# A relu² attention and gated feed-forward kernel on one core: two score buffers and four accumulation banks throughout in place of a shared pair, and an identity matrix zeroed on another engine

## The chip, the cores and the metric

The kernel runs on one core of a Trainium2 chip. A time is the device time of one execution in microseconds (us). "Span" is the time from the first to the last instruction in a profiled execution, without what lies around it.

## The reference

Attention with squared relu for 8 batches of 12 heads, 448 tokens and 64 numbers per head, then a gated feed-forward block over all 3584 tokens:

```python
scores = scale * np.matmul(q, k.transpose(0, 1, 3, 2))      # (8, 12, 448, 448), scale 1/8
attn = np.maximum(scores, 0.0) ** 2 / S                     # S = 448
attn_out = np.matmul(attn, v)
...
x = attn_out.transpose(0, 2, 1, 3).reshape(3584, 768)
g = x @ w_gate                                              # (768, 1536)
gelu = 0.5 * g * (1.0 + erf(g * inv_sqrt2))
val = x @ w_val                                             # (768, 1536)
out = (gelu * val) @ w_out                                  # (1536, 768)
```

## The kernel before

**Tiles of the array.** Every matmul of `mm` (line 160) uses a quarter of TensorE's array, 64 rows by 64 columns. Four can run at once: the lower and the upper half of the rows, each with two column halves. The sum over the upper rows goes on top of that over the lower rows in the same bank of PSUM (the accumulation memory, eight banks), so a bank is first written by "lower" matmuls (plan queue `PE0`), then by "upper" ones (`PE1`). `wait_lower` (line 163) makes the first upper matmul of a bank wait for the last lower one.

**Work per batch**, in the order of the data:

- q and k are loaded by GpSimd's queue (`load_qk`, line 203) and transposed. Batches 0 and 1 use TensorE transposes with the identity matrix `ident` (`add_transposes`, line 358) and a copy by VectorE (line 377). Batches 2 to 7 use a VectorE copy (`qkr`, line 259) and DMA transposes on SyncE's queue (line 263).
- 21 score units per batch (`add_scores`, line 394). A unit's matmuls fill one score buffer `sp` of two banks, ScalarE applies relu (`rl`, line 421) and VectorE squares it (`attnT`, line 427).
- 6 value banks per batch (`add_values`, line 455): attention times v into a bank `ff`, which VectorE scales into `xT` (line 483).
- 24 gate and value banks (`add_gate_value`, line 515): 12 lower and 12 upper matmuls into a bank `ff`. A gate bank is read by gelu on ScalarE (`gel`, line 534), a value bank by VectorE's product (`uT`, line 539).
- 7 output banks per batch on the average (`add_out`, line 568): 24 lower and 24 upper matmuls into a bank `ff`, copied to `osb` (line 594, ScalarE; VectorE for the last tile) and stored by SyncE.

Attention of a batch is mixed with the feed-forward work of the batch before it.

**What sets the order.** The kernel is a plan: each piece is an `Op` with an engine, a cost, the Ops that it needs and a place. `run_plan` (line 23) walks through the queues in planned time and emits the instructions. Lower work has a fixed order (sorted by its place `at`); upper work is sorted by when the lower work ahead of it ends (lines 725 to 742). Both halves are emitted into one instruction queue of TensorE, which executes in order: an instruction that waits holds up all behind it. Until planned time 30, `fill` (line 324) puts dummy matmuls into planned gaps.

**Buffers.** The eight banks are two score buffers of two banks (`psS[0]`, `psS[1]`) and four single banks (`psF`, `FB = 4`). A user of a `psF` bank depends on the reader of the fourth user before it (`ring_dep`, line 338). That holds until the last score unit of batch 1 has been placed (line 442). From then on `next_scores` (line 312) gives all scores to `psS[0]`, each unit waiting for the reader of the one before. `next_bank` (line 298) counts the `ff` users in sixes: four take `psF` banks, the fifth (`n == 0`) allocates one tile of two banks from `psS[1]` and takes its first half, the sixth (`n == 1`) takes the second half of the same tile:

```python
            if half == 0:
                spare_tile[:] = [psS[1].tile([128, 2, 512], f32, name="ff", tag="S")]
            return spare_tile[0][:, half, :]
```

In the plan the fifth user waits for the readers of the pair before, and the sixth for nothing. The tile framework adds its own waits between instructions that touch a tile, in the order in which they are emitted.

**The start.** VectorE clears `warm` and `table` (lines 146, 149); TensorE runs 20 dummy matmuls on `warm` (line 748). GpSimd issues the loads of heads 0 and 1 of q and k, then makes `ident` (`make_identity`, line 628: a memset and a select, lines 197 and 199 of its own file), then issues the loads of heads 2 and 3, and so on (lines 624 to 646).

Of the kernel before, what the change touches and what calls it, by code (L numbers as in the profile page):

```python
# [88 lines left out]
def kernel(  # L89
# [10 lines left out]
    nc = tc.nc  # L100
    f32 = mybir.dt.float32
# [20 lines left out]
    SB = 2  # L122
    FB = 4
# [13 lines left out]
    apool = ctx.enter_context(tc.tile_pool(name="apool", bufs=12))  # L137
    gpool = ctx.enter_context(tc.tile_pool(name="gpool", bufs=3))
    opool = ctx.enter_context(tc.tile_pool(name="opool", bufs=4))
    psS = [ctx.enter_context(tc.tile_pool(name=f"psS{i}", bufs=1, space=bass.MemoryType.PSUM))  # L140
           for i in range(SB)]
    psF = ctx.enter_context(tc.tile_pool(name="psF", bufs=FB, space=bass.MemoryType.PSUM))

    ident = const.tile([128, 128], bf16)
    warm = const.tile([128, 512], bf16)
    nc.vector.memset(warm[:, :], 0.0)

    table = const.tile([128, 2], f32)
    nc.vector.memset(table[:, :], 0.0)
# [135 lines left out]
    ring = [warm_op]  # L285

    in_bank = []
    units, wide, spare, spare_tile = [], [], [[]], []

    def new_bank(reader, shape=(128, 512), dtype=f32, half=None):  # L290
        if half is not None:
            if half == 0:
                spare_tile[:] = [psS[1].tile([128, 2, 512], f32, name="ff", tag="S")]
            return spare_tile[0][:, half, :]
        in_bank.append(reader)
        return psF.tile(list(shape), dtype, name="ff", tag="F")

    def next_bank():

        n = wide[0] % (FB + 2) - FB if wide else -1  # L300
        if wide:
            wide[0] += 1
        if n < 0:
            return None, ring_dep()
        if n == 0:
            spare.append([])
        return n, spare[-2] if n == 0 else []

    def bank_read(half, reader):
        (ring if half is None else spare[-1]).append(reader)  # L310

    def next_scores():

        if wide:
            return 0, units[-1:]
        n = len(units)
        return n % SB, units[n - SB:n - SB + 1]

    def scores_read(n, reader):
        units.append(reader)  # L320
        if n == 1:
            spare[0] = [reader]

    def fill(t0, t1):

# [12 lines left out]
    def ring_dep():  # L338
        return [ring[-FB]] if len(ring) >= FB else []
# [14 lines left out]

    att, xT, last_s = {}, {}, {}
    t_op, relu_op, sq_op, o_op, x_op = {}, {}, {}, {}, {}

    def add_transposes(at, b, m, rs):

        box = {}  # L360

        def emit(r):
            if b == 0:
                t = new_bank(t_op[b, m, r], [128, SC, 2 * P], bf16)
            else:
                if not box:
                    box["S"] = psS[n].tile([128, 2, 1024], bf16, name="sp", tag="S")
                t = box["S"][:, r, 0:SC * 2 * P].rearrange("d (c x) -> d c x", c=SC)
            box[r] = t
            src = qk16[b].rearrange("p (h c d) -> p h c d", c=SC, d=D)  # L370
            for c in range(SC):
                for j in range(2):
                    nc.tensor.transpose(t[HALF[j], c, :], src[:, 2 * (2 * m + r) + j, c, :],  # L373
                                        ident[:, :], tile_position=(0, P * j))

        def emit_copy(r):
            nc.vector.tensor_copy(by_group(qkT_tile(b))[:, m, :, r, :], box[r])

        n, last = next_scores() if b else (0, [])
        for r in rs:  # L380
            have = [*(head_op[b, 2 * m + r, i] for i in range(2)), *(last if b else ring_dep())]
            lo = Op("PE0", 0.5, lambda r=r: emit(r), have, lag=0.2)
            hi = Op("PE1", 0.4, lambda: None)
            hi.after = lo
            t = t_op[b, m, r] = Op("DVE", 0.54, lambda r=r: emit_copy(r),
                                   [lo, last_s.get(b - 2)], lag=0.2, prio=1)
            DVE.append(t)
            if not b:
                ring.append(t)
            both(at, [(lo, hi)])  # L390
        if b:
            scores_read(n, t)

    def add_scores(at, b, u):

# [3 lines left out]
        prs = (2 * m, 2 * m + 1) if tail else (2 * m + (w > VC - 1),)  # L399
        cl = w if w < VC else w - VC  # L400
        box = {}
        n, free = next_scores()

        def emit(j, pr):
            if not box:
                box[0] = psS[n].tile([128, 2, 512], f32, name="sp", tag="S")
            sp = box[0]
            t = by_group(qkT_tile(b))[HALF[j], m, :, pr % 2, :]
            for i in range(2):
                if tail:  # L410
                    n0 = (pr % 2) * S // 2
                    qs = t[:, :, i * P // 2:(i + 1) * P // 2]
                    mm(sp[HALF[i], j, n0:n0 + S // 2].rearrange("k (c p) -> k c p", c=SC),
                       t[:, VC - 1, HALF[1]], qs, j, i, True, True)
                else:
                    mm(sp[HALF[i], j, 0:S].rearrange("k (c p) -> k c p", c=SC),
                       t[:, cl + i * VC, HALF[1]], t[:, :, HALF[0]], j, i, True, True)
# [12 lines left out]
            have = [t_op[b, m, pr % 2] for pr in prs]  # L430
        else:
            have = tr_op[b, m]
        have = [*have, *free]
        ops = [[Op(f"PE{j}", 0.095 if tail else 0.189, lambda j=j, pr=pr: emit(j, pr), have, lag=0.24)
                for pr in prs] for j in range(2)]
        last_s[b] = ops[1][-1]
# [1 line left out]
        n_a = len(sq_list)  # L438
        sq = Op("DVE", 0.54, emit_sq, [relu, *att_free[n_a - 12:n_a - 11]] if n_a >= 12 else [relu],
                lag=0.2, prio=2)  # L440
        scores_read(n, relu)
        if (b, u) == (EARLY - 1, NU - 1):
            wide.append(0)
        sq_list.append(sq)
        att_free.append(None)
        for pr in prs:
# [8 lines left out]
    def add_values(at, b, pr):  # L455
# [1 line left out]

        order = ([0, 3, 1, 2] if pr % 2 else [0, 1, 2, 3], [3, 0, 1, 2])
        last = (b, pr) == (0, NPAIR - 1)
        half, free = next_bank()  # L460

        def emit(i, w):
            if pr == 0 and i == 0 and w == 0:
                xT[b] = xpool.tile([128, KC, S], bf16, name="xT", tag="xT")
            if not box:
                box[0] = new_bank(x_op[b, pr], half=half)
            if (i, w) == (1, VC - 1) or last and (i, w) == (0, 1):
                wait_lower(box)
            for j in range(2):
                o = box[0][HALF[j], 0:S]  # L470
                a = att[b, pr, w][HALF[i], j, :]
                if w < VC - 1:
                    ins = mm(o, v16[b][HALF[i], 2 * pr + j, w + i, :], a, i, j,
                       i == 0 and w == 0, i == 1 - last and w == VC - 2)
                else:
                    ins = mm(o.rearrange("d (c p) -> d c p", c=SC)[:, :, i * P // 2:(i + 1) * P // 2],
                       v16[b][HALF[i], 2 * pr + j, (1 - i) * (VC - 1), :],
                       a[:, (pr % 2) * S // 2:(pr % 2 + 1) * S // 2].rearrange(
                           "k (c p) -> k c p", c=SC), i, j, False, False)
            box[1] = ins  # L480

        def emit_copy():
# [2 lines left out]
        sqs = sq_op[b, pr]  # L485
        have = [head_op[b, pr, 2], head_op[b, pr, 3]]
        ops = [[Op(f"PE{i}", 0.189 if w < VC - 1 else 0.095, lambda i=i, w=w: emit(i, w),
                   [*have, sq_of[b, pr, w], *(free if i == 0 else ())], lag=0.24)
                for w in order[i]]
               for i in range(2)]  # L490
        o_op[b, pr] = ops[1 - last][-1]
# [1 line left out]
            att_free[n_a] = o_op[b, pr]  # L493
        x_op[b, pr] = Op("DVE", 0.54, emit_copy, [o_op[b, pr]], lag=0.2, prio=1)
        DVE.append(x_op[b, pr])
        bank_read(half, x_op[b, pr])
        if last:
            ops[1][0].after = ops[0][1]
            for o, p in zip(ops[1], ops[1][1:]):
# [15 lines left out]
    def add_gate_value(at, b, fc, g):  # L515
# [1 line left out]
        i, o = divmod(fc * 128, WCH)  # L517
        w = (wg, wv)[g][i]
        box = {}
        half, free = next_bank()  # L520

        def emit(r, dc):
            if not box:
                box[0] = new_bank(done, half=half)
            if r == 1 and dc == 0:
                wait_lower(box)
            for j in range(2):
# [8 lines left out]
        def emit_mult():  # L536
            if fc == 0:
# [2 lines left out]
                uT[b][:, fc, :], gel.pop((b, fc))[:, :], box[0][:, 0:S], op=ALU.mult).ins  # L540

        ops = [[Op(f"PE{r}", GS, lambda r=r, dc=dc: emit(r, dc),
                   [w12_op[i][g], x_op[b, dc], *(free if r == 0 and dc == 0 else ())], lag=0.24)
                for dc in range(KC)] for r in range(2)]
        if g == 0:
            done = gel_op[b, fc] = Op("ACT", 0.55, emit_gelu, [ops[1][-1]], lag=0.06, prio=0)
# [1 line left out]
        else:  # L548
# [3 lines left out]
            if b + 2 < B and b:  # L552
# [7 lines left out]
                elif fc > 6:  # L560
                    h0 = 2 * (fc - 7)
                    load_v(b + 2, h0, h0 + 4, [done])
        bank_read(half, done)
        if (b, fc) == (0, 0):
            at = [PLACE5 - 0.5 + 0.1 * g] * 3 + [0.01 * g] * 3
        then(at, GS, *ops, done)
# [1 line left out]
    def add_out(at, t, g):  # L568

        box = {}  # L570
        half, free = next_bank()
        last = 2 * t + 2 == B * SC
        bounds = (0, OGS, OGS + OGS // 2, 2 * OGS) if last else (0, OGS, 2 * OGS)
        cols = slice(bounds[g], bounds[g + 1])
# [3 lines left out]

        def emit(r, fc):
            if not box:  # L580
                box[0] = new_bank(cp, half=half)
            i, o = divmod(fc, WOG)
            if r == 1 and fc == 0:
                wait_lower(box)
# [11 lines left out]
        def emit_store(j, engine, cols):  # L596
# [3 lines left out]

        ops = [[Op(f"PE{r}", step, lambda r=r, fc=fc: emit(r, fc),
                   [wo_op[fc // WOG], *(u_op[b, fc] for b, _ in chunks),
                    *(free if r == 0 and fc == 0 else ())], lag=0.24)
                for fc in range(FC)] for r in range(2)]

        cp = Op("DVE" if last else "ACT", 0.48, emit_copy, [ops[1][-1]], prio=1)
        bank_read(half, cp)
        (DVE if last else ACT).append(cp)
        if t == 0:
            load_qk(2, g, H - 4, H, [cp])  # L610
# [13 lines left out]
    for h0, h1 in ((0, 2), (2, 4), (4, 8), (8, 12)):  # L624
        load_qk(0, 0, h0, h1)
        load_qk(0, 1, h0, h1)
        if h0 == 0:
            POOL.append(Op("POOL", 0.6, lambda: make_identity(nc, ident)))
        if h0 > 2:
            load_v(0, h0 - 4, h1 - 4)  # L630
    load_v(0, 8, 12)
# [77 lines left out]


    def emit_filler():
        t = psS[0].tile([128, 2, 512], f32, name="sp", tag="S")
        for _ in range(2):
            mm(t[HALF[0], 0, 0:P], warm[HALF[0], 0:P], warm[HALF[0], 0:P], 0, 0, True, True)
            mm(t[HALF[1], 0, 0:P], warm[HALF[0], 0:P], warm[HALF[0], 0:P], 0, 1, True, True)
# [68 lines left out]
```

## Time and profile before

| | us |
|---|---|
| three runs | 458.68, 459.71, 460.55 |
| median | 459.71 |
| the profiled execution, its own time | 458.68 |
| its span | 456.7 |
| last matmul ends | 452.64 |
| TensorE busy, of the span | 426.3 |
| VectorE, ScalarE, GpSimd busy | 213.2, 224.3, 73.6 |
| granted TensorE clock | 1.00 in every stretch |

The profile's page sums up one execution. Views of its trace say more: the waits (which engine sat idle, on whose instruction, how long in all, how often, longest), the timeline (instructions in order of time, equal ones merged, with the idle time before them in brackets), groups by form and a table of stretches of time. `ff`, `sp` and the others are the names of tiles; line numbers are those of the kernel before. A matmul row's length includes its way through the array, so rows that follow each other overlap.

### The profile page before, as it was taken

How to read it: one execution, taken by the hardware profiler on the slowest of the kernel's cores; microseconds unless marked ns; L12 is line 12 of the kernel's file. 1: busy time of each engine (PE TensorE's matmuls, PEld its weight loads, DVE VectorE, ACT ScalarE, POOL GpSimd, SP SyncE). 2: the span in 40 equal slices, each digit the busy share in tenths (PEclk: the TensorE clock that was granted, in tenths of full speed). 3: DMA queues.
4: the chain of work that ended last, by engine and by line, in shares of the span. 5: the costliest groups of instructions: out<-in, count | busy, mean ns of one | idle time of the engine just before them, and what ended most of it. 6: DMA issues, size and time to landing. Idle time of an engine off the chain costs nothing.

```text
span 456.7 us, 19664 instructions
## 1 busy us (share of the span) xinstructions
PE 426.3 (93%) x9090; PEld 351.9 (77%) x9090; DVE 213.2 (47%) x347; ACT 224.3 (49%) x320; POOL 73.6 (16%) x120
## 2 busy tenths in 40 slices
PE   8999999999998999998999899989899989999896
PEld 3559679788887888786888788877689877876685
DVE  3967663466434564355534555345543545212201
ACT  4956652656554554554555555554455555221120
POOL 7654302313001130012200121011210000000000
PEclk9999999999999999999999999999999999999999
DMA  8999999988954688637863377544964100220024
GB/s 108 199 197 198 205 187 150 184 103 104 115 91 60 78 112 121 93 43 106 109 141 64 43 106 110 126 62 66 111 119 99 28 1 3 53 56 3 1 72 106
DMA packets 75281, 44.91 MB, mean 98 GB/s; under 512 B 36160, under 2 KB 71744, under 8 KB 75200
## 3 DMA queue, kind: packets, MB, share of 16 engines
q0 software_dynamic: 37152, 24.39, 41.9%
q1 hardware_dynamic: 37888, 19.08, 21.9%
q8 instruction: 71, 1.16, 1.1%
q10 hardware_dynamic: 160, 0.20, 0.1%
q14 instruction: 10, 0.08, 0.1%
HBM read 48.76 MB, written 11.01 MB: 131 GB/s over the span
## 4 chain that ended last, share of the span: by engine, by line
PE 90%; DVE 5%; ACT 2%; DMA 2%; issue 1%; SPq 0%; DVEq 0%; ACTq 0%
PE ff L160 79%; PE sp L160 8%; DVE uT L539 3%; DMA qkT<-qkr 2%; DVE xT L483 2%; PE ff L336 1%; PE ff L748 1%; ACT gel L534 1%; PE ff L373 1%; PE sp L373 1%; ACT osb L594 0%; ACT rl L421 0%; SPq L599 0%; DVE attnT L427 0%; DVE qkr L259 0%
## 5 line engine op out<-in xcount | busy, mean ns | idle before, releaser
L160 PE MATMUL ff<-xT,wg 64*64 64x448 bf16 x2304 | 197.9, 350 | 12.0 <-DVE uT L539 9.9
L421 ACT ACTIVATE rl<-sp 128x896 bf16<-128x896 f32 x168 | 152.3, 918 | 103.7 <-PE sp L160 91.0
L160 PE MATMUL ff<-xT,wv 64*64 64x448 bf16 x2304 | 194.5, 349 | 6.5 <-ACT gel L534 4.3
L160 PE MATMUL ff<-wo,uT 64*64 64x384 bf16 (+1 forms) x2736 | 154.4, 320 | 6.1 <-DVE xT L483 3.3
L160 PEld LDWEIGHTS <-wg 64*64 64x64 bf16 x2304 | 115.2, 107 | 33.8 <-issue 18.3
L427 DVE TENSOR_TENSOR attnT<-rl 128x896 bf16<-128x896 bf16 x168 | 103.8, 622 | 73.5 <-ACT rl L421 71.3
L160 PEld LDWEIGHTS <-uT 64*64 64x64 bf16 x2736 | 120.4, 107 | 18.3 <-issue 9.9
L160 PEld LDWEIGHTS <-wv 64*64 64x64 bf16 x2304 | 116.0, 107 | 23.9 <-issue 10.0
L160 PE MATMUL sp<-qkT 64*64 64x448 bf16 (+1 forms) x768 | 105.8, 328 | 0.5 <-DMA qkT<-qkr 0.3
L539 DVE TENSOR_TENSOR uT<-gel,ff 128x448 bf16<-128x448 bf16 x96 | 59.5, 620 | 90.1 <-PE ff L160 78.5
L160 PE MATMUL ff<-attnT,v 64*64 64x448 bf16 (+1 forms) x768 | 88.4, 326 | 0.1
L534 ACT ACTIVATE gel<-ff 128x448 bf16<-128x448 f32 x96 | 52.0, 542 | 61.3 <-PE ff L160 60.7
L594 ACT COPY osb<-ff 128x384 f32<-128x384 f32 x54 | 25.8, 477 | 59.1 <-PE ff L160 59.0
L160 PEld LDWEIGHTS <-qkT 64*64 64x64 bf16 x768 | 45.0, 106 | 11.6 <-issue 4.3
L483 DVE TENSOR_SCALAR xT<-ff 128x448 bf16<-128x448 f32 x48 | 29.9, 623 | 42.8 <-PE ff L160 42.8
L160 PEld LDWEIGHTS <-v 64*64 64x64 bf16 x768 | 45.7, 107 | 4.8 <-issue 1.1
L212 POOL DMA_DIRECT2D qk<-in_q_dram x25 | 15.5, 621 | 137.6 <-DVE uT L539 117.1
L225 POOL DMA_DIRECT2D v<-in_v_dram x48 | 29.4, 620 | 47.9 <-DVE uT L539 37.9
L212 POOL DMA_DIRECT2D qk<-in_k_dram x25 | 15.4, 615 | 66.7 <-DVE uT L539 59.6
L259 DVE COPY qkr<-qk 128x1792 bf16<-128x1792 bf16 x18 | 19.4, 1078 | 4.6 <-DMA qk<-in_k_dram 4.6
L594 DVE COPY osb<-ff 128x192 f32<-128x192 f32 (+1 forms) x3 | 1.2, 421 | 19.4 <-PE ff L160 19.4
L373 PEld LDWEIGHTS <-qk 128*64 128x64 bf16 x168 | 5.4, 114 | 2.9 <-issue 2.9
(23 smaller groups left out, 43.0 us busy)
## 6 DMA issues: line engine op xcount, KB each, us to landing
out_dram<-osb SPq DMA_DIRECT2D x54, 192.0 KB, 2.7
v<-in_v_dram POOLq DMA_DIRECT2D x48, 128.0 KB, 4.2
qk<-in_q_dram POOLq DMA_DIRECT2D x23, 224.0 KB, 3.9
qk<-in_k_dram POOLq DMA_DIRECT2D x23, 224.0 KB, 4.4
wg<-in_moe_w_gate_dram POOLq DMA_DIRECT2D x6, 384.0 KB, 10.8
wv<-in_moe_w_val_dram POOLq DMA_DIRECT2D x6, 384.0 KB, 11.9
wo<-in_moe_w_out_dram POOLq DMA_DIRECT2D x4, 576.0 KB, 14.8
qkT<-qkr SPq DMA_TRANSPOSE x36, 4.5
```

The lines of the kernel that those rows point to most:

```text
L160: return nc.tensor.matmul(o, lhsT, rhs, start=start, stop=stop, tile_position=(P * row, P * col))
L212: op = load(4 * (h1 - h0) * S * D, lambda: nc.gpsimd.dma_start(tile_of().rearrange("p (h x) -> p h x", h=H)[:, h0:h1, :], src[b, h0:h1].re ...
L225: return nc.gpsimd.dma_start(v16[b][HALF[i], h0:h1, :, :], v[b, h0:h1].rearrange("h (p c) d -> p h c d", c=SC)[:, :, c0:c0 + VC, :])
L259: nc.vector.tensor_copy(qkr[b][:, m], qk16[b].rearrange("p (h c d) -> p c h d", c=SC, d=D)[:, :, 4 * m:4 * m + 4])
L336: nc.tensor.matmul(t[:, :], warm[:, 0:128], warm[:, :], start=True, stop=True)
L373: nc.tensor.transpose(t[HALF[j], c, :], src[:, 2 * (2 * m + r) + j, c, :], ident[:, :], tile_position=(0, P * j))
L421: nc.scalar.activation(rl[:, :, :], box[0][:, :, 0:S], AF.Relu)
L427: nc.vector.tensor_tensor(a[:, :, :], box[1][:, :, :], box[1][:, :, :], op=ALU.mult)
L483: nc.vector.tensor_scalar_mul(xT[b][:, pr, :], box[0][:, 0:S], scalar1=out_scale)
L534: nc.scalar.activation(gel[b, fc][:, :], box[0][:, 0:S], AF.Gelu)
L539: u_op[b, fc].ins = nc.vector.tensor_tensor(uT[b][:, fc, :], gel.pop((b, fc))[:, :], box[0][:, 0:S], op=ALU.mult).ins
L594: cp.ins = (nc.vector.tensor_copy if last else nc.scalar.copy)(osb[t][:, cols], box[0][:, 0:N]).ins
```

## The change

Two things. First, `psS` is one pool of two rotating score buffers for the whole kernel, and every `ff` user takes one of the four `psF` banks; the counting in sixes, the shared two-bank tile and the functions around it are gone. Second, the identity matrix is cleared by VectorE right after `warm`, and GpSimd only does the select (`nomemset=True`), behind the loads of heads 2 and 3 instead of behind those of heads 0 and 1; its planned cost goes from 0.6 to 0.4.

```diff
-    psS = [ctx.enter_context(tc.tile_pool(name=f"psS{i}", bufs=1, space=bass.MemoryType.PSUM))
-           for i in range(SB)]
+    psS = ctx.enter_context(tc.tile_pool(name="psS", bufs=SB, space=bass.MemoryType.PSUM))
...
     nc.vector.memset(warm[:, :], 0.0)
+    nc.vector.memset(ident[:, :], 0.0)
...
-    def new_bank(reader, shape=(128, 512), dtype=f32, half=None):
-        if half is not None:
-            if half == 0:
-                spare_tile[:] = [psS[1].tile([128, 2, 512], f32, name="ff", tag="S")]
-            return spare_tile[0][:, half, :]
+
+    def new_bank(reader, shape=(128, 512), dtype=f32):
         in_bank.append(reader)
         return psF.tile(list(shape), dtype, name="ff", tag="F")
-
-    def next_bank():
-        ...
-    def bank_read(half, reader):
-        (ring if half is None else spare[-1]).append(reader)
-
-    def next_scores():
-        ...
-    def scores_read(n, reader):
-        ...
...
# add_scores (the same in add_transposes)
-        n, free = next_scores()
...
-                box[0] = psS[n].tile([128, 2, 512], f32, name="sp", tag="S")
+                box[0] = psS.tile([128, 2, 512], f32, name="sp", tag="S")
...
-        have = [*have, *free]
+        have = [*have, *units[-SB:1 - SB]]
...
-        scores_read(n, relu)
-        if (b, u) == (EARLY - 1, NU - 1):
-            wide.append(0)
+        units.append(relu)
...
# add_gate_value (the same in add_values and add_out)
-        half, free = next_bank()
...
-                box[0] = new_bank(done, half=half)
+                box[0] = new_bank(done)
...
-                   [w12_op[i][g], x_op[b, dc], *(free if r == 0 and dc == 0 else ())], lag=0.24)
+                   [w12_op[i][g], x_op[b, dc], *(ring_dep() if r == 0 and dc == 0 else ())], lag=0.24)
...
-        bank_read(half, done)
+        ring.append(done)
...
-        if h0 == 0:
-            POOL.append(Op("POOL", 0.6, lambda: make_identity(nc, ident)))
+        if h0 == 2:
+            POOL.append(Op("POOL", 0.4, lambda: make_identity(nc, ident, nomemset=True)))
```

More of the change, by code (lines that the diff above doesn't have):

```diff
@@ L287 @@
     in_bank = []
-    units, wide, spare, spare_tile = [], [], [[]], []
-    def new_bank(reader, shape=(128, 512), dtype=f32, half=None):
-        if half is not None:
-            if half == 0:
-                spare_tile[:] = [psS[1].tile([128, 2, 512], f32, name="ff", tag="S")]
-            return spare_tile[0][:, half, :]
+    def new_bank(reader, shape=(128, 512), dtype=f32):
         in_bank.append(reader)
         return psF.tile(list(shape), dtype, name="ff", tag="F")
-    def next_bank():
[L300 to L307, printed above, removed]
-    def bank_read(half, reader):
-        (ring if half is None else spare[-1]).append(reader)
-    def next_scores():
[L314 to L317, printed above, removed]
-    def scores_read(n, reader):
-        units.append(reader)
-        if n == 1:
-            spare[0] = [reader]
     def fill(t0, t1):
@@ L356 @@
     t_op, relu_op, sq_op, o_op, x_op = {}, {}, {}, {}, {}
+    units = []
     def add_transposes(at, b, m, rs):
@@ L366, in emit @@
                 if not box:
-                    box["S"] = psS[n].tile([128, 2, 1024], bf16, name="sp", tag="S")
+                    box["S"] = psS.tile([128, 2, 1024], bf16, name="sp", tag="S")
                 t = box["S"][:, r, 0:SC * 2 * P].rearrange("d (c x) -> d c x", c=SC)
@@ L377, in emit_copy @@
             nc.vector.tensor_copy(by_group(qkT_tile(b))[:, m, :, r, :], box[r])
-        n, last = next_scores() if b else (0, [])
+        last = units[-SB:1 - SB]
         for r in rs:
@@ L391, in add_transposes @@
         if b:
-            scores_read(n, t)
+            units.append(t)
     def add_scores(at, b, u):
@@ L465, in emit @@
             if not box:
-                box[0] = new_bank(x_op[b, pr], half=half)
+                box[0] = new_bank(x_op[b, pr])
             if (i, w) == (1, VC - 1) or last and (i, w) == (0, 1):
@@ L487, in add_values @@
         ops = [[Op(f"PE{i}", 0.189 if w < VC - 1 else 0.095, lambda i=i, w=w: emit(i, w),
-                   [*have, sq_of[b, pr, w], *(free if i == 0 else ())], lag=0.24)
+                   [*have, sq_of[b, pr, w], *(ring_dep() if i == 0 else ())], lag=0.24)
                 for w in order[i]]
@@ L495, in add_values @@
         DVE.append(x_op[b, pr])
-        bank_read(half, x_op[b, pr])
+        ring.append(x_op[b, pr])
         if last:
@@ L519, in add_gate_value @@
         box = {}
-        half, free = next_bank()
         def emit(r, dc):
             if not box:
-                box[0] = new_bank(done, half=half)
+                box[0] = new_bank(done)
             if r == 1 and dc == 0:
@@ L570, in add_out @@
         box = {}
-        half, free = next_bank()
         last = 2 * t + 2 == B * SC
@@ L580, in emit @@
             if not box:
-                box[0] = new_bank(cp, half=half)
+                box[0] = new_bank(cp)
             i, o = divmod(fc, WOG)
@@ L602, in add_out @@
                    [wo_op[fc // WOG], *(u_op[b, fc] for b, _ in chunks),
-                    *(free if r == 0 and fc == 0 else ())], lag=0.24)
+                    *(ring_dep() if r == 0 and fc == 0 else ())], lag=0.24)
                 for fc in range(FC)] for r in range(2)]
         cp = Op("DVE" if last else "ACT", 0.48, emit_copy, [ops[1][-1]], prio=1)
-        bank_read(half, cp)
+        ring.append(cp)
         (DVE if last else ACT).append(cp)
@@ L711, in emit_filler @@
     def emit_filler():
-        t = psS[0].tile([128, 2, 512], f32, name="sp", tag="S")
+        t = psS.tile([128, 2, 512], f32, name="sp", tag="S")
         for _ in range(2):
```

## The prediction, on record before the result

> **What bounds the kernel now.** I read the page first, then the waits, then the timeline where TensorE waits, then stretches of time by engine and by form of matmul. The page and the waits:
>
> ```profile
> PE 426.3 (93%) x9090; PEld 351.9 (77%) x9090; DVE 213.2 (47%) x347; ACT 224.3 (49%) x320; POOL 73.6 (16%) x120
> ```
>
> ```profile
> PE ff L160 <- DVE uT L539: 11.2, 18, 0.8
> PE ff L160 <- DVE xT L483: 7.5, 11, 0.7
> ...
> PE ff L160 <- ACT gel L534: 4.3, 7, 0.7
> ...
> PE ff L160 <- ACT osb L594: 1.4, 3, 0.6
> ```
>
> TensorE (PE) is the bound: 93% busy, no other engine at half. Of its 30.4 us of idle time (456.7 - 426.3), these four rows hold 11.2 + 7.5 + 4.3 + 1.4 = 24.4 us, in 18 + 11 + 7 + 3 = 39 waits. The rest is the start (1.2 us) and the last copy and store (456.7 - 452.6 = 4.1 us). In all four rows TensorE waits for the reader of an `ff` bank. The timeline near the end, where nothing but gate and value banks runs, shows what kind of wait it is (start, length, instruction; in brackets the idle time before it):
>
> ```profile
> 410.94 1.48 PE L160 MATMUL ff<-xT,wg 64*64 64x448 bf16 x24
> 412.08 1.48 PE L160 MATMUL ff<-xT,wv 64*64 64x448 bf16 x24
> 413.21 1.48 PE L160 MATMUL ff<-xT,wg 64*64 64x448 bf16 x24
> 414.35 1.48 PE L160 MATMUL ff<-xT,wv 64*64 64x448 bf16 x24
> 415.48 0.73 PE L160 MATMUL ff<-xT,wg 64*64 64x448 bf16 x10
> 416.99 0.94 PE L160 MATMUL ff<-xT,wg 64*64 64x448 bf16 x14 [0.78 <-DVE uT L539]
> ```
>
> A bank's worth of 24 matmuls starts every 1.135 us ((415.48 - 410.94) / 4). At 415.48 TensorE issues only 10 of 24, stops, and goes on when the product `uT` (VectorE, 416.31 to 416.93) has ended. The same rows stand at 409.21 and 424.77: the stop comes back every 7.78 us. Counting the instructions that read `ff` banks (`gel`, `uT`, `osb`, `xT`) between one such stop and the next gives six, nearly everywhere from 84 us on; in three places it is 12 or 13, one stop being missing or short. Six is the cycle of `next_bank`, whose fifth and sixth user share one tile. The stop is in the middle of a bank, where TensorE has already been writing, so it isn't a wait for a free bank. I read it as a wait inside the pair: the matmuls of the second half that are emitted after the reader of the first half wait for that reader, since both are the same tile, and the whole queue waits with them.
>
> Before the pair exists, two score buffers and four banks serve the same mixture, which is what the change makes of the whole kernel. The stretches (length; PE busy, instructions; PEld; DVE; ACT; POOL; clock; DMA share; GB/s):
>
> ```profile
> 35.00:45.00 10.00, 10.00 (x226) 9.40 (x224) 7.07 (x13) 6.56 (x9) 4.64 (x6) 1.00 1.41 198
> 45.00:55.00 10.00, 10.00 (x222) 6.83 (x216) 6.54 (x12) 5.89 (x8) 4.76 (x7) 1.00 1.36 203
> 55.00:65.00 10.00, 10.00 (x226) 6.91 (x220) 6.70 (x12) 7.27 (x10) 0.00 (x0) 1.00 1.18 208
> ...
> 125.00:175.00 50.00, 46.53 (x1006) 40.61 (x1002) 24.45 (x41) 26.22 (x37) 7.32 (x12) 1.00 0.67 88
> ```
>
> With four banks TensorE has no idle time from 35 to 65 us, though VectorE is 65 to 71% busy there and 49% later. With the pair it idles 3.5 of 50 us.
>
> **The sum.** Against the profiled execution: span 456.7, own time 458.68; the median of the runs is 459.71, 1.03 above it.
>
> *Idle stops removed: -24.4 us*, the four rows. All of it is on the path, since TensorE's queue is in order and the bound. What would be late next is TensorE's own next matmul.
>
> *Emptying and refilling at each stop: -7.4 us.* At the tail six banks should take 6 x 1.135 = 6.81 us and take 7.78: 0.97 lost, of which 0.78 is shown idle. The other 0.19 is time in which the array ran partly empty. 39 x 0.19 = 7.4. Bounds: nothing, and by the groups by form from 130 to 182 us: 720 matmuls of 64x448 at 1.135/24 = 0.0473, 286 of 64x384 at 0.0407 (288 of them, six output banks, in 11.9 - 0.2 us behind 432.49) and 48 of 64x224 at 0.0237 need 46.8 of 52 us. So 5.2 are lost there, 3.5 of them idle, 1.7 not; over 370 us that would be 12. I take the tail's, the one that a stop shows by itself.
>
> *Waits for one of four banks, in place of one of six: +4 us.* No row shows four banks with the output matmuls and with the `qkr` copies of later batches. Lower bound: nothing, as from 35 to 65 us. A bank's life with the upper half right behind the lower is 2 x 1.135 + 0.35 (a matmul's way through) + 0.1 + 0.62 (the reader) = 3.3 us; four banks come round in 4 x 1.135 = 4.54, so a reader may be 1.2 us late. One `attnT` product ahead of it (0.62) fits, one `qkr` copy (1.08) just so, both don't: 0.5 us over. If that met each of the 18 `qkr` copies, 9 us; if further readers met two in front as well, 20. An output bank has 1.95 us of matmuls, so those come round more slowly. I take 4, nearer to the stretch that has no such wait.
>
> *Two score buffers instead of one: nothing.* In the whole list of waits TensorE waits for a relu once, 0.2 us, at 16 us, with two buffers; the single one later has cost it no idle time.
>
> *The identity: -0.3 us.* The rows of the start:
>
> ```profile
> 1.95 0.61 POOL L212 DMA_DIRECT2D qk<-in_k_dram  x1
> ...
> 2.54 0.23 POOL masks.py:197 MEMSET ident<- 128x128 bf16 x1
> 2.85 0.29 POOL masks.py:199 TENSOR_SCALAR_AFFINE_SELECT ident<-ident 128x128 bf16<-128x128 bf16 x1
> ...
> 3.09 0.59 POOL L212 DMA_DIRECT2D qk<-in_q_dram  x1
> ...
> 5.04 0.18 PEld L373 LDWEIGHTS <-qk 128*64 128x64 bf16 x2 [0.25 <-issue]
> ```
>
> The third and fourth load move up by 0.55 us (3.09 to 2.54), all later ones on GpSimd's queue by the memset, about 0.23. VectorE's memset costs between 0.06 (`table`) and 0.27 (`warm`, four times as wide in words), 0.1 by size; it stands ahead of `table`, whose only user on ScalarE first has a table load until 2.02. The select then ends near 3.75 + 0.35 = 4.1, and TensorE first uses `ident` behind the dummy matmuls, at 5.04 to 5.46: 0.9 us of cover. Without it each us would be added to the start. The gain lies between nothing (dummy matmuls fill the start) and 0.55, if loads set the start of the feed-forward work at 25.2; I take 0.3.
>
> Transposes: nothing new is late. The DMA transposes of batch 2 land at 80.2, ahead of the first stop, as now; those of batch 3 are issued from 95 us on for scores from 122.6 on, over 20 us ahead.
>
> Sum: -24.4 - 7.4 + 4 - 0.3 = -28.1. The profiled execution would take 430.6, the median 459.71 - 28.1 = **431.6 us**.
>
> A rule speaks against this. The Trainium skill ("Perfetto Trace Analysis", Optimization Strategy) says that the same gap coming back on the engine that should be saturated can mean too few buffers in SBUF or PSUM. By that the gap every 7.8 us would call for more banks, and taking two of six would lengthen it. The trace doesn't agree: the stop falls behind the tenth matmul of a bank, not ahead of its first, and four banks from 35 to 65 us show none.
>
> **The rivals.**
>
> *Four banks are short in part* (chance 0.14). Readers late behind `qkr` and `attnT`, in the stage with output banks. For it: from 65 us on no row shows it. Against: the 30 us at higher load of VectorE. Price 9 to 20 in place of 4: 436 to 448.
>
> *Four banks are short everywhere, slower than before* (0.03). If the plan lets the upper half run two banks behind the lower, a bank's life is 3 x 1.135 + 0.35 + 0.1 + 0.62 = 4.5 us of 4.54. Then each product or relu ahead of a reader stops TensorE. Some 260 `ff` banks follow 65 us; from 32.1 / 260 = 0.12 us a bank on the gain is gone. With one product ahead of every fourth reader (0.62 / 4 = 0.15 a bank) it is 39 us: 459.7 - 32.1 + 39 = 467. Against: 35 to 65 us again.
>
> *The stops aren't those of the pair* (0.02), the reader of every sixth bank being late by itself: then they stay, 459. Against: stops before 65 us are missing, and readers of four kinds on two engines are named in a cycle of six.
>
> *All unseen loss goes as well* (0.06): -24.4 - 12 - 0.5, and no new wait: 422.
>
> **How the numbers follow.** Forecast with its bounds, 424 to 440: 0.75. The rivals: 0.14, 0.03, 0.02, 0.06. The range 424 to 444 leaves out the upper half of the first rival (0.07), the slow one, no change and most of the last: 0.17. What a measurement can tell from no change is about 0.5%, 2.3 us. Faster by more than that: 0.75 + 0.14 + 0.06 = 0.95; the same: 0.02; slower: 0.03.
>
> **What would show it.** Right: the four rows of waits shrink to a few us with no cycle of six; the tail's gate banks run 24 by 24 at 1.135 us with no `[0.78 <-DVE uT L539]`; TensorE's busy share goes to 97% or more from 75 us on. Wrong: stops ahead of a bank's first matmul, after `qkr` copies above all (first rival); waits of the same kind in every bank (second); the same stops every sixth bank (third). For the identity: a third load at 2.5 us and no wait of TensorE for `ident`.

## The result and the profile after

The changed kernel takes 428.06 us (median of four runs, 427.36 to 428.50) against 460.13 (four runs of the kernel before, 458.68 to 462.65). The ratio is 0.930, 95% interval 0.925 to 0.934: 32 us faster, inside the range of 424 to 444. One execution of the kernel before, taken beside ident_only below, lasted 1574 us and is left out of the ratios.

The profiled execution: own time 428.50, span 426.7. The page, engines over the span:

```profile
PE 419.4 (98%) x9090; PEld 358.4 (84%) x9090; DVE 213.0 (50%) x348; ACT 223.6 (52%) x320; POOL 73.5 (17%) x119
```

The number of matmuls is the same, 9090. TensorE's busy time is 6.9 us less (426.3 to 419.4) and its idle time 23.1 less (30.4 to 7.3), which makes the 30.0 us of the span. The waits of TensorE, all that the list has (`warm` is the start; `uT` now has line 504):

```profile
PE ff L712 <- DVE warm L145: 1.2, 1, 1.2
PE sp L160 <- DMA qkT<-qkr: 1.1, 1, 1.1
PE ff L160 <- DVE uT L504: 0.6, 1, 0.6
PE sp L160 <- ACT rl L390: 0.2, 1, 0.2
```

Of the 39 waits for readers of `ff` banks (24.4 us) one is left, 0.6 us. The stretches of time, in the same columns as before (PE busy and instructions come second):

```profile
75.00:125.00 50.00, 48.26 (x1070) 42.48 (x1064) 27.93 (x44) 29.31 (x41) 10.73 (x18) 1.00 1.14 143
125.00:175.00 50.00, 50.00 (x1118) 44.16 (x1112) 27.02 (x43) 28.96 (x41) 7.32 (x12) 1.00 0.66 95
175.00:225.00 50.00, 50.00 (x1124) 46.28 (x1118) 26.14 (x41) 26.87 (x41) 7.32 (x12) 1.00 0.67 106
...
325.00:375.00 50.00, 50.00 (x1117) 44.22 (x1112) 22.27 (x38) 25.87 (x38) 0.00 (x0) 1.00 0.14 34
```

From 125 us to its last matmul, which ends at 422.7, TensorE has no idle time, and does 1118 matmuls in the 50 us in which it did 1006. The tail, where only gate and value banks are left, now runs without a break. VectorE's timeline there shows it best, one `uT` for each pair of banks:

```profile
384.81 0.62 DVE L504 TENSOR_TENSOR uT<-gel,ff 128x448 bf16<-128x448 bf16 x1 [1.65 <-PE ff L160]
387.08 0.62 DVE L504 TENSOR_TENSOR uT<-gel,ff 128x448 bf16<-128x448 bf16 x1 [1.65 <-PE ff L160]
389.35 0.62 DVE L504 TENSOR_TENSOR uT<-gel,ff 128x448 bf16<-128x448 bf16 x1 [1.65 <-PE ff L160]
```

They come every 2.27 us, which is 2 x 1.135, in the whole stretch from 382 to 399 us. Before, the same instruction had this rhythm:

```profile
411.40 0.62 DVE L539 TENSOR_TENSOR uT<-gel,ff 128x448 bf16<-128x448 bf16 x1 [2.24 <-PE ff L160]
413.67 0.62 DVE L539 TENSOR_TENSOR uT<-gel,ff 128x448 bf16<-128x448 bf16 x1 [1.65 <-PE ff L160]
416.31 0.62 DVE L539 TENSOR_TENSOR uT<-gel,ff 128x448 bf16<-128x448 bf16 x1 [2.03 <-PE ff L160]
```

The product at 416.31 should have begun at 415.94 (413.67 + 2.27). It waited as well: it began 0.1 us after the end of the ten matmuls that TensorE issued before it stopped (415.48 + 0.73 = 416.21). In the program's order four of the ten belong to the second half of the tile and six to another bank; the product reads none of them. So the shared tile held up both sides. The reader of the first half waited for the matmuls of the second half that had been emitted ahead of it, and then the other matmuls of the second half waited for that reader. The waits in the program agree: in the tail a shared tile gets 48 matmuls, 24 for either half. The 36th is the last of the first half, the reader of that half waits for the 40th, and the 41st waits for VectorE.

What is left in the changed kernel stands at 80 us:

```profile
78.65 1.09 DVE L259 COPY qkr<-qk 128x1792 bf16<-128x1792 bf16 x1 [5.00 <-DMA qk<-in_k_dram]
...
79.66 0.61 DVE L504 TENSOR_TENSOR uT<-gel,ff 128x448 bf16<-128x448 bf16 x1
...
80.32 0.57 PE L160 MATMUL ff<-xT,wv 64*64 64x448 bf16 x8 [0.64 <-DVE uT L504]
...
82.00 0.38 PE L160 MATMUL sp<-qkT 64*64 64x448 bf16 x2 [1.11 <-DMA qkT<-qkr]
```

A `qkr` copy stands ahead of a bank's reader, and TensorE waits 0.64 us for that bank; then it waits 1.11 us for the first DMA transposes of batch 2.

### The profile page after: what moved, and what is told of

It is laid out like the page before. It is cut to its first block, busy times and chain, and to the rows that moved or that the text cites. A ratio compares the mean times of both kernels' runs of the same rounds, so it can differ in the third digit from the quotient of the medians.

```text
span 426.7 us, 19600 instructions
## 1 busy us (share of the span) xinstructions
PE 419.4 (98%) x9090; PEld 358.4 (84%) x9090; DVE 213.0 (50%) x348; ACT 223.6 (52%) x320; POOL 73.5 (17%) x119
## 4 chain that ended last, share of the span: by engine, by line
PE 96%; DMA 2%; ACT 0%; SPq 0%; DVE 0%; issue 0%
PE ff L160 84%; PE sp L160 8%; DMA qkT<-qkr 2%; PE ff L305 1%; PE ff L712 1%; PE ff L343 1%; PE sp L343 1%; SPq L563 0%; ACT rl L390 0%; ACT osb L558 0%; DVE osb L558 0%; DVE warm L145 0%
## 5 line engine op out<-in xcount | busy, mean ns | idle before, releaser
L160 PE MATMUL ff<-xT,wv 64*64 64x448 bf16 x2304 | 217.1, 349 | 0.6 <-DVE uT L504 0.6
L160 PE MATMUL ff<-xT,wg 64*64 64x448 bf16 x2304 | 217.3, 349 | 0.0
L160 PE MATMUL ff<-wo,uT 64*64 64x384 bf16 (+1 forms) x2736 | 150.7, 320 | 0.0
L160 PEld LDWEIGHTS <-wv 64*64 64x64 bf16 x2304 | 125.7, 107 | 16.9 <-issue 2.2
L160 PEld LDWEIGHTS <-wg 64*64 64x64 bf16 x2304 | 125.2, 107 | 16.5 <-issue 0.5
L160 PEld LDWEIGHTS <-uT 64*64 64x64 bf16 x2736 | 125.9, 107 | 5.4 <-issue 0.6
L160 PE MATMUL sp<-qkT 64*64 64x448 bf16 (+1 forms) x768 | 108.7, 328 | 1.3 <-DMA qkT<-qkr 1.1
L160 PE MATMUL ff<-attnT,v 64*64 64x448 bf16 (+1 forms) x768 | 86.1, 326 | 0.1
L160 PEld LDWEIGHTS <-qkT 64*64 64x64 bf16 x768 | 43.6, 106 | 11.2 <-issue 4.5
```

What stands on the lines that cost most here:

```text
L160: return nc.tensor.matmul(o, lhsT, rhs, start=start, stop=stop, tile_position=(P * row, P * col))
```

## The experiments

Theory A: the two halves of one tile wait for each other's instructions, and that is the loss. Theory B: six banks and one score buffer are a bad division by themselves; the upper half of the array runs further behind, and readers come late. The kernel before had both, so the change alone can't tell them apart. The first four ran on one chip, where the kernel before took 459.89 us.

**pair_split.** The kernel before with two tiles in place of two halves; the pool of the second score buffer is closed at the first use of the pair and a pool of two single banks opened in its place. This is the part of the edit that matters:

```diff
-            if half == 0:
-                spare_tile[:] = [psS[1].tile([128, 2, 512], f32, name="ff", tag="S")]
-            return spare_tile[0][:, half, :]
+            if not psX:
+                one.close()
+                psX.append(ctx.enter_context(tc.tile_pool(name="psX", bufs=2, space=bass.MemoryType.PSUM)))
+            return psX[0].tile(list(shape), dtype, name="ff", tag="X")
```

> The kernel before, except that the fifth and the sixth ff user take two tiles of one bank each in place of the halves of one tile of two banks. Still six banks, one score buffer and the old identity from batch 2 on. Theory A (the halves of one tile wait for each other's instructions): no stop every sixth bank, TensorE waits for ff readers under 3 us in all, 428 to 431 us, ratio 0.932 to 0.937. Theory B (it is the arrangement of six banks and one score buffer, which lets the upper half run further behind and readers come late): the stops stay, 455 to 460 us.

Measured: 425.65 us, ratio 0.925 (0.921 to 0.930), a little better than expected. TensorE's waits:

```profile
PE sp L162 <- DMA qkT<-qkr: 1.5, 1, 1.5
PE ff L751 <- DVE table L151: 1.2, 1, 1.2
PE ff L376 <- DMA qk<-in_k_dram: 0.5, 2, 0.3
PE sp L162 <- ACT rl L424: 0.2, 1, 0.2
```

No wait for an `ff` reader is left. With all else of the kernel before in place (six banks, one score buffer, the old identity), separate tiles bring the whole gain. The two programs issue the same 9090 matmuls in the same order, so the order of the plan can't be the cause. Theory B falls.

**pair_in_10** and **halves_apart_10.** The shared tile stays, but serves two of every ten users in place of two of every six: 26 tiles in place of 43. In the first kernel they are neighbours, in the second four other banks lie between them.

```diff
-        n = wide[0] % (FB + 2) - FB if wide else -1
+        n = (-1, -1, -1, -1, -1, -1, -1, -1, 0, 1)[wide[0] % 10] if wide else -1   # pair_in_10
+        n = (-1, -1, -1, -1, 0, -1, -1, -1, -1, 1)[wide[0] % 10] if wide else -1   # halves_apart_10
```

> The kernel before, with the shared tile used for users nine and ten of every ten in place of five and six of every six: 26 shared tiles in place of 43. Theory A: the loss goes with the number of shared tiles. (460.1 - 428.4) / 43 = 0.74 us each, so 428.4 + 26 x 0.74 = 447.6, 445 to 450 us, and a stop every ten readers. Theory B: six banks and one score buffer are still there, 455 to 460 us.

> As pair_in_10, 26 shared tiles, but the two halves are users five and ten of every ten, so that four other banks lie between them. Theory A in its narrow form (the wait costs only because the neighbour's reader has just begun): by the time of the second half the reader of the first is long done, 428 to 433 us, no cycle of ten in the stops. Theory A in its wide form (a shared tile costs a stop wherever its halves stand): as pair_in_10, 445 to 450 us. Theory B: 455 to 460 us.

Measured: 448.50 us (ratio 0.976, 0.970 to 0.982) and 425.91 us (0.927, 0.920 to 0.933). The waits for `ff` readers of pair_in_10, then the longest waits of halves_apart_10:

```profile
PE ff L160 <- DVE uT L539: 6.9, 11, 0.8
PE ff L160 <- DVE xT L483: 3.8, 6, 0.7
PE ff L160 <- ACT gel L534: 2.2, 4, 0.6
PE ff L160 <- ACT osb L594: 1.6, 4, 0.6
```

```profile
PE sp L160 <- DMA qkT<-qkr: 1.6, 1, 1.6
PE ff L748 <- DVE table L149: 1.2, 1, 1.2
PE ff L160 <- issue: 0.3, 1, 0.3
```

pair_in_10 has 25 such waits for 26 tiles, and ten readers of `ff` banks between one and the next nearly everywhere. Against pair_split it loses 22.9 us, 0.88 a tile; the kernel before loses 34.2, 0.80 a tile. So the loss goes with the number of neighbouring pairs. halves_apart_10 has the same 26 shared tiles, the matmul order of the kernel before, and none of these waits: in its tail the reader of the first half ends 1.5 us before the second half is first written. Sharing a tile costs nothing by itself. It costs when the two halves are in work at the same time.

**banks_only.** The changed kernel with the old identity.

> The changed kernel with the old identity (GpSimd clears it and finishes it behind the first two loads): the change of buffers alone. Theory A: all but 0.2 us of the gain is here, 428.3 us, ratio 0.930 to 0.934; the first scores at 7.00 us in place of 6.81. Rival (the identity carries a part through the loads): 430 us or more.

Measured: 427.78 us, ratio 0.930 (0.925 to 0.935). The change of buffers is the whole gain. Its time is 2.1 us above that of pair_split on the same chip, and all four of its runs are above all four of pair_split.

**ident_only.** The kernel before with the new identity. This one, three_banks, qk2_first and after_again ran together on one chip, where the kernel before took 459.99 us.

> The kernel before with the new identity alone. Theory: 0.2 us less than before in the trace (first scores at 6.81 us, first gate matmul at 24.98 in place of 25.17), which a comparison of times can't show; ratio 0.997 to 1.002. Rival (earlier loads shorten the stage that the loads set): over 1 us, ratio under 0.997.

Measured: 459.26 us, ratio 0.9997 (0.997 to 1.002). GpSimd's timeline has the third load at 2.55 us, as in the changed kernel:

```profile
1.95 0.61 POOL L213 DMA_DIRECT2D qk<-in_k_dram  x1
2.55 0.61 POOL L213 DMA_DIRECT2D qk<-in_q_dram  x1
3.13 0.62 POOL L213 DMA_DIRECT2D qk<-in_k_dram  x1
3.81 0.34 POOL masks.py:199 TENSOR_SCALAR_AFFINE_SELECT ident<-ident 128x128 bf16<-128x128 bf16 x1
```

The loads are issued earlier, but the first gate matmul comes at 25.32 us. It comes at 25.18 in the kernel before, 25.14 in banks_only and 25.16 in pair_split (old identity), at 24.99, 25.51 and 25.21 in three profiles of the changed kernel. The start varies by more than the identity could give.

**three_banks.** The changed kernel with one `ff` bank less.

```diff
-    FB = 4
+    FB = 3
```

> The changed kernel with three ff banks in place of four; one bank is unused. A bank's life in the changed kernel's tail is 3.8 to 4.0 us of the 4.54 in which four come round; three come round in 3.40. Theory (four are just enough, and the plan can shorten a life only by letting lower matmuls wait): waits for a reader ahead of most banks, 0.1 to 0.4 us each on 260 banks, 450 to 530 us. Rival (the order of the plan adapts and the upper half follows more closely): under 440 us.

Measured: 491.26 us, ratio 1.068 (1.064 to 1.072): 63.5 us over the changed kernel on that chip (after_again), 0.2 us for each of some 310 banks. Its main waits:

```profile
PE sp L160 <- ACT rl L390: 9.7, 18, 0.8
PE ff L160 <- DVE uT L504: 4.6, 13, 0.7
PE ff L160 <- ACT gel L499: 1.9, 8, 0.3
```

They make 16 us. With the smaller ones TensorE's idle time is 26.6 us, 19.3 more than in the changed kernel. The other 43.7 us are busy time: 463.1 us in place of 419.4, for the same work. The stops that were expected ahead of most banks didn't come: 26 waits for `ff` readers are in the list. The loss sits in the order instead. In the plan the lower matmuls wait for a bank while upper ones go on, so that one half of the array runs empty, which the profile counts as busy: in the tail a pair of banks takes 2.50 us in place of 2.27, and TensorE shows no idle time there. Four banks are needed in this plan; what two more bring is asked below.

**after_again** is the base on that chip.

> The changed kernel once more, as the base for the others on this chip: 427.4 to 428.5 us, ratio 0.93.

Measured: 427.78 us, ratio 0.931 (0.928 to 0.934). Its profile has no wait for the DMA transposes of batch 2, where the first profile has 1.1 us, after_third below 1.0, and the two of pair_split 1.5 and 0.8: when they land differs from one execution to the next.

**qk2_first** goes after that wait. The loads for the first transposes of batch 2 are put ahead of the last output weights.

```diff
-    for i in range(FC // WOG):
+    for i in range(FC // WOG - 1):
         load_wo(i)
-
-    for m in range(NM - 1):
+    for i in range(2):
+        load_qk(2, i, 0, 4)
+    load_wo(FC // WOG - 1)
+    for m in range(1, NM - 1):
```

> The changed kernel with the loads of heads 0 to 3 of q and k of batch 2 ahead of the last load of the output weights, to have the first DMA transposes land before TensorE asks for them at 81 us. If that wait is the only thing there: its 1.1 us and up to 0.6 of a stop next to it go, 426.3 to 427.5 us. Rival (the output weights come late instead): TensorE waits for wo near 66 us, 428 to 430 us.

Measured: 428.57 us, ratio 0.931 (0.928 to 0.934), no gain, and 1.1 us over the upper end of what was expected. There is no wait for `qkT`, but after_again beside it has none either, so the profile doesn't show what the edit does to it. A wait of 0.4 us for `wo` is new, as the rival had it.

**split_ident**, **pair_split_2** and **after_third**: a version that would beat both kernels, these three again together on one chip (kernel before 459.57 us). split_ident is pair_split with the new identity.

> pair_split with the new identity: six single banks and one score buffer from batch 2 on, and the identity of the change. Theory (six single banks give up to 2 us over four, since the changed kernel loses about 5.2 us to partly empty array from 85 to 395 us and pair_split 3.0; the identity gives nothing that can be seen): 425 to 426.5 us, ratio to the kernel before 0.924 to 0.928. Rival (the 2 us were the scatter between profiles and chips): as the changed kernel on this chip, within 0.3 us.

> pair_split again beside the changed kernel on the same chip. Theory: 425.0 to 426.0 us, 1 to 3 us under the changed kernel. Rival: within 0.5 us of it.

> The changed kernel on the same chip, the base for these two: 427.3 to 428.5 us.

Measured: 426.11 us (0.9275, 0.924 to 0.931), 426.53 us (0.9275, 0.924 to 0.931) and 428.40 us (0.931, 0.928 to 0.934). Six single banks were ahead of four by 2.3 and 1.9 us here, and by 2.1 us in pair_split against banks_only above. The medians lean the same way three times, and the profiles say where the time is: TensorE is busy for 416.1 to 416.5 us in the four with six banks and no stops (halves_apart_10 among them), for 418.6 to 419.4 in the five with four. The intervals of the ratios overlap, though: the best version found is about 0.5% faster than the changed kernel, and that is at the edge of what these runs can tell.

## Why the prediction was right, step by step

- **Idle stops removed, -24.4.** Right: 0.6 of the 24.4 us is left, in one wait. The cause was right too, a wait inside the pair (pair_split, halves_apart_10). What it missed is that the reader of the first half is held up as well, by 0.4 us at the tail.
- **Emptying and refilling, -7.4.** The effect is there, and the size came out close partly by luck. TensorE's busy time fell by 6.9 us, but two things are in that. pair_split, with the same matmuls in the same order as the kernel before and no stops, fell by 9.9 (426.3 to 416.4). So the stops cost 0.25 us each on the average beside their idle time, where the tail's shows 0.19; the bound of 12 was nearer than the 7.4. The changed kernel then gives 3.0 of it back (next item).
- **Waits for one of four banks, +4.** The size fits, the form does not. Idle time rose by 0.6 only, the one stop at 80.32; its cause is the one named, a `qkr` copy ahead of a reader, but it came once and not at many of the 18 copies. The rest of the price is in busy time: 419.4 us against 416.4 in pair_split, 3.0 more for the same work. From 85 to 395 us neither has idle time, and the changed kernel does 6895 matmuls where pair_split does 6941. That makes 3.6 us in these two profiles; the medians side by side differ by 1.9 to 2.3. The working behind the term failed too. It took a bank's life as 3.3 us, with the upper half right behind the lower. With the program's order laid beside the trace, in the changed kernel's tail a gate bank lives 3.8 us from its first matmul to the end of gelu, a value bank 3.96 to the end of the product, and the upper half starts 1.7 banks behind the lower. So it does run further behind, as the rival of the slow side feared, and the fourth user after such a bank starts only 0.58 to 0.73 us after its reader has ended. It is still in time, since the plan counts the four banks and orders the work by them. Three banks, 3.40 us for such a life, lose 63.5 us: too few banks can make the kernel slower than it was, as that rival said, but mostly by a partly empty array and not by stops.
- **Two score buffers, nothing.** Right; relu holds up TensorE once, 0.2 us, in both kernels.
- **Identity, -0.3.** In the two profiles the first scores come 0.19 us earlier (7.00 to 6.81), but other profiles scatter by more (6.29 and 7.24 with the old identity, 6.65 and 7.24 with the new), and ident_only shows no difference. Not confirmed.
- **DMA transposes, nothing new late.** Not quite: in this profile they land at 82.0 in place of 80.2 and cost 1.1 us in place of 0.3. after_again has no such wait, so the change alone doesn't bring it; what sets their time wasn't looked into.
- **The sum.** -28.1 forecast, -30.0 in the spans. By the measured terms, 2.5 more come from the emptying (-9.9), 0.4 more from the four banks (+3.6), and 0.8 go the other way for the transposes: -28.1 - 2.5 - 0.4 + 0.8 = -30.2. A small slip is in the rival in which all unseen loss goes: its terms give 422.8 us, not 422. The medians differ by 32.1, more than the profiled executions, of which the one before is the fastest of its runs and the one after the slowest.
- **The rule for recurring gaps** (the Trainium skill, "Perfetto Trace Analysis", Optimization Strategy) would have asked for more banks. The trace disagrees here: the same six banks without the sharing have no such gap (pair_split), and with two banks less one wait of 0.6 us is left in place of 39. That too few banks can cost much shows in three_banks, 63.5 us.

## What to carry to other kernels

When a gap comes back at a fixed count of tiles, look where it falls. Here it fell in the middle of a bank that was already being written, which spoke against too few buffers and for a wait between two things that have nothing to do with each other. Two accumulations in work at the same time should be two tiles, even where one allocation would hold both. Whether buffers are enough is asked of the stretch that already runs with that number; a life estimated from durations misses how far the plan lets one half run behind.

## What the runs showed of the hardware

A TensorE that the profile shows as busy isn't a full array: three_banks is 95% busy (463.1 of 489.7 us) and 15% slower than the changed kernel for the same work, and the busy time of the kernel before held 9.9 us more than that of pair_split for the same matmuls in the same order. The weight loads' share tells more here: 77% before, 84% after, 89% in pair_split, 74% in three_banks. The granted clock was 0.997 to 1.00 in all runs of the changed kernel, although TensorE had no idle time for nearly 300 us. Small differences of that clock show in the times: beside ident_only the kernel before took 458.7 to 461.0 us at mean clocks of 0.997 to 1.00, and 462.7 to 463.0 at 0.994 and 0.995.
